# Attention and a mixer branch on one core: the first bit piece written from PSUM, twelve more shared blocks, and row-tile scores for some own key tiles

## The chip, the cores and the metric

The kernel runs on one NeuronCore of a Trainium2 chip. The metric is the device time of one execution in microseconds; lower is better. Before the change the median of three runs is 877.18 us (876.33 to 880.28). A core has five engines that run side by side and meet at semaphores: TensorE (PE, matrix products into PSUM), ScalarE (ACT, table functions such as exp and GELU), VectorE (DVE, elementwise work), GpSimd (POOL) and SyncE (SP, which here issues the DMA transfers). PSUM has eight banks of 512 fp32 columns on 128 partitions.

## The reference

```python
x  = A_x                                   # (1, 2048, 640) bf16
xn = layernorm(x)
# A: attention, 32 heads of 20
q, k, v = split(xn @ wqkv)                 # wqkv (640, 1920)
p = softmax(q @ k.T * 20**-0.5)            # 2048 x 2048 per head
s = concat_heads(p @ v) @ wo
# B: a mixer with two GELU products
h  = gelu(layernorm(xn) @ w1)              # four quarters of h are shifted by
hs = shift(h) @ w2                         # +1, -1, +2, -2 positions
x1 = xn + hs
g  = silu(x1 + gelu(layernorm(x1) @ w3) @ w4)   # w3 (640, 1536)
out = x + s * g
```

The exponentials are the bulk of it: 32 heads times 2048 x 2048 scores. On 128 partitions they are 1024 tiles of 128 x 1024.

## The kernel before

Heads are taken four at a time (a quad; eight of them), queries 512 at a time (a chunk; four per quad). Scores come with the keys on the partitions, so a key tile of 128 keys, with four heads and 512 queries, fills two PSUM tiles of 128 x 1024. For most key tiles ScalarE exponentiates both. A shared block is a pair of key tiles of which ScalarE takes one half and VectorE the other.

The kernel describes its work as tasks. A list scheduler inside the kernel, which runs when the program is built, puts the tasks of each engine into a fixed order, assigns PSUM banks and buffers, and adds the semaphore waits. `DUE` and some other numbers steer that order.

```python
self.RESERVE = 500.0
self.AHEAD = 3
# by number of shared blocks in a chunk: (position, block in unit, blocks of unit)
self.UNITS = ((),
              ((3, 0, 1),),
              ((0, 0, 2), (2, 1, 2)),
              ((0, 0, 2), (2, 1, 2), (7, 0, 1)),
              ((0, 0, 2), (1, 1, 2), (3, 0, 2), (5, 1, 2)))
self.ND = ([1, 2, 3, 3], [4, 4, 4, 3], [3, 3, 3, 2], [3, 3, 4, 3],   # shared blocks of
           [3, 2, 4, 2], [4, 3, 4, 4], [3, 3, 4, 3], [4, 4, 3, 1])   # each quad's chunks
# ...
EXP_B = (0.25, 32.25, 64.75, 96.75)
EXP_W = (1.0, 1.0, 181.0 / 256.0, 181.0 / 256.0)
EXP_BIAS = 31951.2055
# ... PSUM: bank 7 holds the weighted sum, banks 0 to 6 are shared
pairs = [(0, [0, 1]), (0, [2, 3])]
high = [(0, [4, 5]), (0, [5, 6]), (1, [4, 6])]
pl.kind("W", "B", [(0, [4]), (0, [6]), (1, [5])])             # projections, B branch
pl.kind("S", "B", pairs)                                      # one ScalarE tile
pl.kind("SD", "B", [(r + q, x + y) for r, x in pairs for q, y in high] + ...)
```

[...]a linear map of the score, read as a bf16 pattern, is 2 to a power with a linear mantissa. Four such patterns, shifted against each other by a fraction of an octave, two of them with a weight, add up to a smoother approximation. The sum is not formed on VectorE: each pattern (a piece) is a TensorE operand of its own, weighted through a scaled copy of V (`VP`). Before, the PSUM pass writes the linear map at twice the resolution into U, and each of four SBUF passes halves it and adds its piece's offset.

```python
def block_bits(self, quad, qc, blocks, ends):
    w = 2048 * len(blocks)
    # ...
    for v in range(4):
        k = self.piece % 3
        self.piece += 1
        dst, dsta = SS[:, k, 0:w], [A("SS", k)]
        T("dve", ..., lambda e, v=v, dst=dst: e.tensor_scalar(dst, U[:, ub, 0:w], 0.5, EXP_B[v], op0=ALU.mult, op1=ALU.add), ...)  # L1482
        for n, (j, kts) in enumerate(blocks):
            # four matmuls, one per head, each in its own column tile        # L1491
            ins = e.matmul(pb[32 * i:32 * i + 22, 0:512], wv, dst[:, at:at + 512].bitcast(BF16), ..., tile_position=(0, 32 * i))

def score(self, e, out, b, qc, kt, i):                     # row tile: 32 partitions of one head
    return e.matmul(out, self.KT[32 * i:32 * i + 32, b, 128 * kt:128 * kt + 128],
                    self.QT[32 * i:32 * i + 32, b, 512 * qc:512 * qc + 512],
                    start=True, stop=True, tile_position=(32 * i, 0))       # L1499

def score_act(self, b, qc, kt, a, gb=None):                # an own key tile, half a of two
    hs, sa = self.stile()
    def fn(e):
        for jj in range(2):
            out = self.bank(hs.slot + jj)
            if gb is None:                                 # first chunk of all: row tiles
                ins = self.score(e, out[:, :], b, qc, kt, 2 * a + jj)
                continue
            for c in range(4):                             # otherwise: QM is zero outside a head
                ins = e.matmul(out[32 * c:32 * c + 32, :], self.KT[:, b, 128 * kt + 32 * c:128 * kt + 32 * c + 32],
                               self.QM[:, gb, 2 * a + jj, :], start=True, stop=True, tile_position=(0, 32 * c))  # L1517
        return ins
    T("pe", ..., acq=("S", hs))
    return self.exp_act(hs, sa)                            # 128 x 1024 exponentials, L1541

def score_both(self, b, qc, kt, a, quad, r):               # half of a block: four row tiles at once
    # ... two heads to hs (ScalarE), two to hd (VectorE); four banks, acq=("SD", hs, hd)
    slot = self.exp_act(hs, sa)
    # the PSUM pass, L1568
    ins = e.tensor_scalar(U[:, ub, ...], self.psum[:, ...], a_exp, EXP_BIAS, op0=ALU.mult, op1=ALU.add)
```

Line numbers to know: L787 is every projection and B branch product; L1364 the weighted sum of ScalarE's tiles; L1405 the scores of the last chunk, which is done in two halves of 256 queries; L1603 takes a chunk's weighted sum out of PSUM; L1840 and L1911 are GELUs, L1927 the tanh of the gate.

Of the kernel before, what the change touches and what calls it, by code (L numbers as in the profile page):

```python
# [610 lines left out]
class Cfg:  # L611
# [5 lines left out]
    def __init__(self, S=2048, D=640, H=32, F=1536):  # L617
        self.S, self.D, self.H, self.F = S, D, H, F
        self.DH = D // H
        assert self.DH == 20 and D % 128 == 0 and F % 128 == 0 and S % 512 == 0  # L620
        self.NT = S // 128
        self.NQC = S // 512
        self.KC = D // 128
        self.FC = F // 128
        self.NQUAD = H // 4
        self.QW = 4 * self.DH
        self.scale = self.DH ** -0.5
        self.OFFSET = 60.0
        self.T0 = 38000.0
        self.STEP = 960.0  # L630
        self.DUE = dict(
            k0=-48.1, k1=-97.0, k2=-104.6, k3=-121.0, k4=-126.4, v0=25.8, v0s=11.55, v1=995.9, v1s=14.38, w1=349.3,
            w1s=18.63, g1=819.9, x1=141.8, x1s=0.43, wo=-14.8, st=92.5, g3_0=638.9, g3_2=540.7, si_0=348.9, si_2=654.6,
            sis=20.68, u0=4.5, s0=1.0, u1=3.5, s1=40.8, u2=-8.6, s2=51.1, u3=-29.2, s3=20.1, u4=-26.8, s4=-17.2, u5=-23.0,
            s5=-20.2, u6=-29.6, s6=-8.2, u7=-32.5, s7=170.4, mx=-11.2, mxs=3.13)
        self.BLK = [(2, 3), (6, 7), (10, 11), (14, 15)]
        self.RESERVE = 500.0
        self.POOLN = [0, 9, 14]
        self.HPE = 0.0
        self.HDVE = 0.0  # L640
        self.THIRD = False
        self.FALL = True
        self.SAVE = 1
        self.AHEAD = 3
        self.UNITS = ((),
                      ((3, 0, 1),),
                      ((0, 0, 2), (2, 1, 2)),
                      ((0, 0, 2), (2, 1, 2), (7, 0, 1)),
                      ((0, 0, 2), (1, 1, 2), (3, 0, 2), (5, 1, 2)))
        self.HPS = 6  # L650
        self.FILL = 0
        self.LNA = [3, 3]
        self.VAFTER = 6
        self.NPF = [34, 8]
        self.TRA = [1, 2, 3, 4, 8, 13, 17, 18]
        self.ONP = 0
        self.LAST = [[[4, 2]], []]
        self.ND = (
            [1, 2, 3, 3],
            [4, 4, 4, 3],  # L660
            [3, 3, 3, 2],
            [3, 3, 4, 3],
            [3, 2, 4, 2],
            [4, 3, 4, 4],
            [3, 3, 4, 3],
            [4, 4, 3, 1])

    def order(self, quad, qc):

        nb = self.ND[quad][qc]
        used = [k for b in self.BLK[:nb] for k in b]
        ks = [k for k in range(self.NT) if k not in used]
        at = {}
        for j, (pos, r, n) in enumerate(self.UNITS[nb]):
            at.setdefault(pos, []).append(("b", j, r, n))
        out = []
        for i in range(len(ks) + 1):
            out += at.pop(i, [])  # L680
            if i < len(ks):
                out.append(("k", ks[i]))
        assert not at
        return out

# [1 line left out]

EXP_B = (0.25, 32.25, 64.75, 96.75)  # L690
EXP_W = (1.0, 1.0, 181.0 / 256.0, 181.0 / 256.0)
EXP_BIAS = 31951.2055


def c_dve(n, kind="psum"):
# [11 lines left out]
def c_act(n):  # L707
    return 68 + 0.8333 * n
# [13 lines left out]
class Gen:  # L722
# [71 lines left out]
    def build(self, plan_only=False):  # L794
        nc, pl = self.nc, self.pl
        with contextlib.ExitStack() as es:
# [13 lines left out]
            pl.kind("S", "B", pairs + (third if self.cfg.THIRD else []))  # L810
            pl.kind("SD", "B", [(r + q, x + y) for r, x in pairs for q, y in high]
                    + ([(3, pairs[0][1] + pairs[1][1]), (3, pairs[1][1] + pairs[0][1])] if self.cfg.FALL else []))
            pl.hold = {"pe": self.cfg.HPE, "dve": self.cfg.HDVE}
            if self.cfg.SAVE:
                pl.saves = {"SD": "W"}
                pl.reserve = self.cfg.RESERVE
                pl.hard = self.cfg.SAVE == 2
            pl.pool("PT", 7)
            self.program()
            ms = pl.schedule(verbose=True)  # L820
            if plan_only:
# [497 lines left out]
    def attn_quad(self, quad):  # L1319
# [9 lines left out]
        for qc in range(NQC):  # L1329
# [17 lines left out]
            for kind, x, *unit in seq:  # L1347
                if kind == "k":
                    slots = [self.score_act(b, qc, x, a, gb if col else None) for a in range(2)]
                    kts = (x, x)  # L1350
                else:
                    ka, kb = kts = cfg.BLK[x]
                    r, n = unit
# [22 lines left out]
    def last_half(self, quad, qc, half, gb):  # L1376
# [40 lines left out]
        for x, kt in enumerate(ks):  # L1417
# [9 lines left out]
            for unit in at.get(x, []):  # L1427
# [3 lines left out]
                for m, kx in enumerate(unit):  # L1431
                    hs, sa = scores(kx, "d")
                    T("dve", c_dve(1024),
                      lambda e, m=m, hs=hs, ub=ub: e.tensor_scalar(U[:, ub, 1024 * m:1024 * m + 1024], self.psum[:, 512 * hs.slot:512 * hs.slot + 1024],
                                                                   cfg.scale * math.log2(math.e) * 256.0, EXP_BIAS, op0=ALU.mult, op1=ALU.add),
                      reads=[sa], writes=[A("U", ub, m)], name=f"uh{half}_{kx}", rel=hs, cls=-1 - half, due=self.at(self.nact, f"u{quad}"))
                for v in range(4):
                    k = self.piece % 3
                    self.piece += 1
                    T("dve", c_dve(w, "4x"),  # L1440
                      lambda e, v=v, k=k, ub=ub, w=w: e.tensor_scalar(SS[:, k, 0:w], U[:, ub, 0:w], 0.5, EXP_B[v], op0=ALU.mult, op1=ALU.add),
                      reads=[A("U", ub, m) for m in range(len(unit))], writes=[A("SS", k)], name=f"s_h{half}_{unit[0]}_{v}", cls=-2 * half,
                      due=self.at(self.nact, f"s{quad}"))
                    for m, kx in enumerate(unit):
                        own = EXP_W[v] == 1.0
                        T("pe", c_pe(4, 256), pv(vown if own else (lambda j, i: VX[:, j // 2, i, :]), kx,
                                                 lambda i, k=k, m=m: SS[:, k, 1024 * m + 256 * i:1024 * m + 256 * i + 256].bitcast(BF16)),
                          reads=[A("SS", k), A("VX") if not own else A(f"VA{hf}", kx), pva], name=f"pvd_h{half}_{kx}_{v}", cls=-half)
            T("pe", c_pe(4, 256), pv(vown, kt, lambda i, hp=hp: PT[:, hp.slot, 256 * i:256 * i + 256]), reads=[pa, A(f"VA{hf}", kt), pva], rel=hp,
              name=f"pv_h{half}_{kt}", cls=-1)  # L1450
        RZ, Ob, h8 = self.RZ, self.Ob, 8 * half
# [16 lines left out]
    def block_bits(self, quad, qc, blocks, ends):  # L1468
# [7 lines left out]
        self.unit += 1  # L1476
        halves = [A("U", ub, k) for k in range(2 * len(blocks))]
        for v in range(4):
            k = self.piece % 3
            self.piece += 1  # L1480
            dst, dsta = SS[:, k, 0:w], [A("SS", k)]
            T("dve", c_dve(w, "4x"), lambda e, v=v, dst=dst: e.tensor_scalar(dst, U[:, ub, 0:w], 0.5, EXP_B[v], op0=ALU.mult, op1=ALU.add),  # L1482
              reads=halves, writes=dsta, name=f"s{quad}_{qc}_{blocks[0][0]}_{v}", due=self.at(self.nact, f"s{quad}"))
            for n, (j, kts) in enumerate(blocks):
                def fn(e, v=v, dst=dst, n=n, j=j, kts=kts):
                    pb = self.bank(self.PVB)
# [15 lines left out]
    def score_act(self, b, qc, kt, a, gb=None):  # L1502
# [19 lines left out]
          writes=[sa, ("turn", self.step)], name=f"sc{self.step}", mode=int(gb is None), cls=-1, acq=("S", hs))  # L1522
        return self.exp_act(hs, sa)

    def stile(self):
        h = Handle()
        a = ("S", h.id)
# [19 lines left out]
    def score_both(self, b, qc, kt, a, quad, r):  # L1547
# [4 lines left out]
        U, ub = self.U, self.unit % 2  # L1552
        o = 1 - a
        at = 2 * r + o
        a_exp = cfg.scale * math.log2(math.e) * 256.0
        (hs, sa), (hd, da) = self.stile(), self.stile()
        def fn(e):
            for i in range(4):
# [410 lines left out]
```

## Time and profile before

| | before |
|---|---|
| time, median of three | 877.18 us |
| span of the profiled run | 873.5 us |
| TensorE matmuls | 16078, busy 830.2 us |
| VectorE busy | 732.3 us |
| ScalarE busy | 837.9 us |
| first exponential starts | 36.9 us |
| mean granted TensorE clock | 0.993 |

Busy time is how long an engine had an instruction in flight. On TensorE instructions overlap and their ends are modelled, so its share doesn't tell how much room is left; the distance from the start of one instruction to the start of the next does. A row of the groups gives line, engine and operation, output and input shapes, count, then busy microseconds and mean nanoseconds of one, then the idle time of the engine ahead of it and what ended it. In a list of waits the numbers are microseconds in total, times, and the longest one. In the chain that ended last each stretch belongs to the work that the next one had to wait for.

### The profile page before, as it was taken

How to read it: one execution, taken by the hardware profiler on the slowest of the kernel's cores; microseconds unless marked ns; L12 is line 12 of the kernel's file. 1: busy time of each engine (PE TensorE's matmuls, PEld its weight loads, DVE VectorE, ACT ScalarE, POOL GpSimd, SP SyncE). 2: the span in 40 equal slices, each digit the busy share in tenths (PEclk: the TensorE clock that was granted, in tenths of full speed). 3: DMA queues.
4: the chain of work that ended last, by engine and by line, in shares of the span. 5: the costliest groups of instructions: out<-in, count | busy, mean ns of one | idle time of the engine just before them, and what ended most of it. 6: DMA issues, size and time to landing. Idle time of an engine off the chain costs nothing.

```text
span 873.5 us, 35127 instructions
## 1 busy us (share of the span) xinstructions
PE 830.2 (95%) x16078; PEld 373.4 (43%) x16078; DVE 732.3 (84%) x1006; ACT 837.9 (96%) x887; POOL 43.6 (5%) x74
## 2 busy tenths in 40 slices
PE   7899989999999999999999999999998999999996
PEld 3334333333344444443444545444333344443485
DVE  7746779999879998889886599799997778899957
ACT  7699999999999999999999999999999999999994
POOL 7600000000000000000110000000000000000000
PEclk9999999999999999999999999999999999999998
DMA  7001533222130001331323112232221202013232
GB/s 227 17 2 36 130 88 88 77 84 84 57 92 13 26 26 45 104 75 35 76 53 99 32 55 84 78 98 53 61 52 46 60 26 70 25 48 113 84 95 92
DMA packets 86483, 59.06 MB, mean 68 GB/s; under 512 B 53056, under 2 KB 77840, under 8 KB 86336
## 3 DMA queue, kind: packets, MB, share of 16 engines
q1 hardware_dynamic: 86336, 56.82, 23.6%
q8 instruction: 126, 2.06, 1.0%
q14 instruction: 21, 0.17, 0.1%
HBM read 42.10 MB, written 10.63 MB: 60 GB/s over the span
## 4 chain that ended last, share of the span: by engine, by line
ACT 74%; PE 16%; DVE 7%; DMA 2%; issue 1%; SPq 0%
ACT arena L1541 70%; PE psum L787 6%; PE psum L1517 3%; ACT arena L1911 2%; PE psum L1499 2%; PE psum L1405 2%; PE psum L1364 1%; DVE arena L1568 1%; DVE arena L1482 1%; PE psum L1491 1%; ACT arena L1927 1%; DMA queries<-arena 1%; DMA arena<-in_A_x_dram 1%; DMA recips<-arena 1%; DVE arena L1199 1%
## 5 line engine op out<-in xcount | busy, mean ns | idle before, releaser
L1541 ACT ACTIVATE arena<-psum 128x1024 bf16<-128x1024 f32 x826 | 769.1, 1038 | 9.5 <-PE psum L1499 3.4
L787 PE MATMUL psum<-arena 128*32 128x320 bf16 (+1 forms) x5952 | 358.3, 333 | 6.0 <-DVE arena L1201 3.0
L1517 PE MATMUL psum<-arena 128*32 128x512 bf16 x4576 | 348.2, 381 | 7.8 <-ACT arena L1541 6.5
L1568 DVE TENSOR_SCALAR arena<-psum 128x1024 uint16<-128x1024 f32 x196 | 238.7, 1218 | 39.4 <-PE psum L1499 39.0
L1482 DVE TENSOR_SCALAR arena<-arena 128x4096 uint16<-128x4096 uint16 (+1 forms) x228 | 238.1, 1070 | 3.6 <-PE psum L1491 2.5
L787 PEld LDWEIGHTS psum<-arena 128*32 128x32 bf16 x5952 | 148.2, 96 | 138.4 <-issue 25.8
L1517 PEld LDWEIGHTS psum<-arena 128*32 128x32 bf16 x4576 | 97.3, 95 | 130.8 <-ACT arena L1541 93.5
L1364 PE MATMUL psum<-arena 128*22 128x512 bf16 x1592 | 152.0, 380 | 0.8 <-DVE arena L1603 0.6
L1491 PE MATMUL psum<-arena 128*22 128x512 bf16 x1568 | 129.1, 380 | 0.6 <-DVE arena L1482 0.6
L1499 PE MATMUL psum<-arena 32*128 32x512 bf16 x840 | 88.0, 385 | 13.0 <-ACT arena L1541 6.8
L1499 PEld LDWEIGHTS psum<-arena 32*128 32x128 bf16 x840 | 22.4, 91 | 102.1 <-ACT arena L1541 80.9
L1364 PEld LDWEIGHTS psum<-arena 128*22 128x22 bf16 x1592 | 40.3, 92 | 49.1 <-issue 6.8
L1491 PEld LDWEIGHTS psum<-arena 128*22 128x22 bf16 x1568 | 36.6, 92 | 43.5 <-issue 8.6
L1907 DVE CAST arena<-psum 128x512 bf16<-128x512 f32 x48 | 32.8, 684 | 11.6 <-PE psum L787 10.1
L1245 DVE CAST arena<-psum 128x512 bf16<-128x512 f32 x40 | 27.3, 685 | 18.1 <-PE psum L787 17.9
L1691 DVE SCALAR_TENSOR_TENSOR arena<-psum,arena 128x320 bf16<-128x320 f32 x32 | 15.4, 486 | 13.8 <-PE psum L787 13.7
L1922 DVE TENSOR_TENSOR arena<-psum,arena 128x320 bf16<-128x320 f32 x32 | 15.5, 485 | 13.3 <-PE psum L787 12.2
L999 DVE BATCH_NORM_STATS2 arena<-arena 128x6 f32<-128x320 bf16 x52 | 22.9, 480 | 3.3 <-DMA arena<-in_A_x_dram 3.2
L1314 POOL TENSOR_SCALAR arena<-arena 128x176 bf16<-128x176 bf16 x16 | 8.5, 534 | 326.1 <-DVE arena L1306 326.0
L1306 DVE CAST arena<-psum 128x320 bf16<-128x320 f32 x32 | 15.1, 487 | 10.9 <-PE psum L787 10.9
L1603 DVE COPY arena<-psum 128x512 f32<-128x512 f32 x28 | 19.2, 685 | 2.7 <-PE psum L1491 1.7
L1616 DVE TENSOR_TENSOR arena<-arena 128x512 bf16<-128x512 f32 x28 | 19.1, 683 | 2.1 <-DMA arena<-recips 2.1
(118 smaller groups left out, 349.1 us busy)
## 6 DMA issues: line engine op xcount, KB each, us to landing
arena<-in_B_w_dram SPq DMA_DIRECT2D x48, 160.0 KB, 2.6
arena<-recips SPq DMA_DIRECT2D x28, 256.0 KB
arena<-arena SPq DMA_DIRECT2D x124, 32.0 KB, 1.9
arena<-in_B_w_dram SPq DMA_DIRECT2D x4, 960.0 KB, 5.8
arena<-in_A_x_dram SPq DMA_DIRECT2D x8, 320.0 KB, 6.2
arena<-in_A_x_dram SPq DMA_DIRECT2D x16, 160.0 KB, 2.5
out_dram<-arena SPq DMA_DIRECT2D x16, 160.0 KB, 1.9
heads<-arena SPq DMA_DIRECT2D x112, 20.0 KB
```

The costliest lines, as they stand in the source:

```text
L787: ins = e.matmul(pb[32 * c:32 * c + 32, 0:N], lhsT(k, c), rhs(k, c), start=(k == 0), stop=(stop and k == nk - 1), tile_position=(0, 32 * c))
L999: lambda e, li=li, n=n, hh=hh: e.bn_stats(st[:, li, 6 * hh:6 * hh + 6], xn[:, n, hD * hh:hD * hh + hD]),
L1245: T("dve", c_dve(512), lambda e, h=h, c=c: e.tensor_copy(KS[:, 512 * c:512 * c + 512], self.wbank(h)[:, 0:512]), reads=[wa], writes=[A("KS ...
L1364: ins = e.matmul(pb[32 * i:32 * i + 22, 0:512], VA[:, ql, kts[i // 2], i, :], PT[:, slots[i // 2][0].slot, 512 * (i % 2):512 * (i % 2) + 512],
L1482: T("dve", c_dve(w, "4x"), lambda e, v=v, dst=dst: e.tensor_scalar(dst, U[:, ub, 0:w], 0.5, EXP_B[v], op0=ALU.mult, op1=ALU.add), reads=ha ...
L1491: ins = e.matmul(pb[32 * i:32 * i + 22, 0:512], wv, dst[:, at:at + 512].bitcast(BF16), start=first, stop=final, tile_position=(0, 32 * i))
L1499: return e.matmul(out, self.KT[32 * i:32 * i + 32, b, 128 * kt:128 * kt + 128], self.QT[32 * i:32 * i + 32, b, 512 * qc:512 * qc + 512], s ...
L1517: ins = e.matmul(out[32 * c:32 * c + 32, :], self.KT[:, b, 128 * kt + 32 * c:128 * kt + 32 * c + 32], self.QM[:, gb, 2 * a + jj, :], start ...
L1541: lambda e: e.activation(self.PT[:, hp.slot, :], self.psum[:, 512 * hs.slot:512 * hs.slot + 1024], AF.Exp, scale=cfg.scale),
L1568: ins = e.tensor_scalar(U[:, ub, 1024 * at + 512 * k:1024 * at + 512 * k + w], self.psum[:, 512 * hd.slots[k]:512 * hd.slots[k] + w], a_ex ...
L1603: T("dve", c_dve(512), lambda e: e.tensor_copy(Ob[:, :], self.bank(self.PVB)[:, :]), writes=[("PV", 0), A("Ob")], name=f"ob{quad}_{qc}", c ...
L1907: T("dve", c_dve(512), lambda e, h=h, fc=fc, i=i: e.tensor_copy(GT[:, i, fc, :], self.wbank(h)[:, 0:512]), reads=[wa], writes=at, name=f"g ...
```

## The change

Four things change together. The linear map is written at single resolution, with the first piece's offset in it, so the PSUM pass yields the first piece itself: TensorE reads it straight from U, and three SBUF passes, each a single add, make the other three. Shared blocks go from 98 to 110, so VectorE takes 24 more of the 1024 tiles and ScalarE 24 fewer. 39 own key tiles (outside the first chunk) take their scores in one set of four row tiles, as blocks do, instead of 16 matmuls against QM: 31 of them with two exponentials of 1024, and eight ("w") with one exponential of 2048 over four adjacent banks. And the numbers that steer the scheduler are other ones, so the order of tasks is another one nearly everywhere. In the first chunk no block is shared any more.

```diff
-            k0=-48.1, k1=-97.0, k2=-104.6, ...
+            k0=553.73, k1=-179.82, k2=-347.19, ...
...
-        self.RESERVE = 500.0
+        self.RESERVE = 350.0
...
-        self.AHEAD = 3
+        self.AHEAD = 2
...
+        self.NR = (
+            [[], [12, 110, 113], [5, 11, 105, 108, 112, 114], [3, 6, 9, 10, 11, 106, 112, 114]],
...
         self.ND = (
-            [1, 2, 3, 3],
-            [4, 4, 4, 3],
-            [3, 3, 3, 2],
-            [3, 3, 4, 3],
-            [3, 2, 4, 2],
+            [0, 4, 4, 3],
+            [4, 4, 4, 4],
+            [3, 2, 4, 4],
             [4, 3, 4, 4],
-            [3, 3, 4, 3],
-            [4, 4, 3, 1])
+            [3, 4, 4, 4],
+            [4, 3, 4, 4],
+            [3, 4, 4, 4],
+            [4, 4, 2, 3])
...
+        rows = self.NR[quad][qc]
...
-                out.append(("k", ks[i]))
+                out.append(("r" if i in rows else "w" if 100 + i in rows else "k", ks[i]))
...
-EXP_B = (0.25, 32.25, 64.75, 96.75)
+EXP_B = (0.0, 32.0, 64.0, 96.0)
 EXP_W = (1.0, 1.0, 181.0 / 256.0, 181.0 / 256.0)
-EXP_BIAS = 31951.2055
+EXP_BIAS = 15975.95
...
+            pl.kind("SR", "B", [(r + q, x + y) for r, x in pairs for q, y in high[:2]]
+                    + [(3, pairs[0][1] + pairs[1][1]), (3, pairs[1][1] + pairs[0][1])])
+            pl.kind("SW", "B", [(0, [2, 3, 4, 5])])
...
         for v in range(4):
-            k = self.piece % 3
-            self.piece += 1
-            dst, dsta = SS[:, k, 0:w], [A("SS", k)]
-            T("dve", c_dve(w, "4x"), lambda e, v=v, dst=dst: e.tensor_scalar(dst, U[:, ub, 0:w], 0.5, EXP_B[v], op0=ALU.mult, op1=ALU.add),
-              reads=halves, writes=dsta, name=f"s{quad}_{qc}_{blocks[0][0]}_{v}", due=self.at(self.nact, f"s{quad}"))
+            if v == 0:
+                dst, dsta = U[:, ub, 0:w], halves
+            else:
+                k = self.piece % 3
+                self.piece += 1
+                dst, dsta = SS[:, k, 0:w], [A("SS", k)]
+                T("dve", c_dve(w, "4x"), lambda e, v=v, dst=dst: e.tensor_scalar(dst, U[:, ub, 0:w], EXP_B[v], None, op0=ALU.add),
+                  reads=halves, writes=dsta, name=f"s{quad}_{qc}_{blocks[0][0]}_{v}", due=self.at(self.nact, f"s{quad}"))
...
+    def score_rows(self, b, qc, kt, wide):
+        tiles = [self.stile() for _ in range(2)]
+        def fn(e):
+            for i in range(4):
+                ins = self.score(e, self.bank(tiles[i // 2][0].slots[i % 2])[:, :], b, qc, kt, i)
+            return ins
+        T("pe", 220, fn, ..., acq=("SW" if wide else "SR",) + tuple(h for h, _ in tiles))
+        if not wide:
+            return [self.exp_act(h, a) for h, a in tiles]
...
+        T("act", c_act(2048),
+          lambda e: e.activation(self.PT[:, hp[0].slot:hp[0].slot + 2, :], self.psum[:, 512 * h0.slot:512 * h0.slot + 2048]...,
+                                 AF.Exp, scale=self.cfg.scale), ...)
...
-        a_exp = cfg.scale * math.log2(math.e) * 256.0
+        a_exp = cfg.scale * math.log2(math.e) * 128.0
```

## The prediction

> **What bounds the kernel now.** I read the page's first part, then the chain that ended last, then ScalarE's waits, then the costly groups, then TensorE in order of time.
>
> ```profile
> PE 830.2 (95%) x16078; PEld 373.4 (43%) x16078; DVE 732.3 (84%) x1006; ACT 837.9 (96%) x887; POOL 43.6 (5%) x74
> ...
> ACT 74%; PE 16%; DVE 7%; DMA 2%; issue 1%; SPq 0%
> ```
>
> ScalarE is busy for 96% of the span and is 74% of the chain. TensorE's 95% is not a margin read directly, because matmuls overlap in the records; I come back to it. ScalarE's waits, from first exponential to last (37 to 860 us):
>
> ```profile
> ACT arena L1541 <- PE psum L1499: 3.4, 7, 1.1
> ACT arena L1541 <- PE psum L1364: 3.0, 3, 2.1
> ACT arena L1541 <- PE psum L1405: 2.0, 1, 2.0
> ACT arena L1541 <- PE psum L1517: 0.5, 2, 0.4
> ```
>
> In those 823 us ScalarE is busy for 813.9 and waits 9 us, always for TensorE. By windows, 4.2 us of it lie between 100 and 200 us, 2.1 us at 420 to 440 and 2.0 us at 820 to 840. So an exponential taken from ScalarE is worth nearly its whole slot, as long as TensorE and VectorE keep up. The groups:
>
> ```profile
> L1541 ACT ACTIVATE arena<-psum 128x1024 bf16<-128x1024 f32 x826 | 769.1, 1038 | 9.5 <-PE psum L1499 3.4
> ...
> L1568 DVE TENSOR_SCALAR arena<-psum 128x1024 uint16<-128x1024 f32 x196 | 238.7, 1218 | 39.4 <-PE psum L1499 39.0
> ```
>
> One exponential lasts 1038 ns, but 826 of them make 769.1 us of busy time: they overlap, and the slot is 769.1 / 826 = 931 ns. The bit passes, shapes kept apart:
>
> ```profile
> L1482 DVE TENSOR_SCALAR arena<-arena 128x4096 uint16<-128x4096 uint16 x164 | 196.3, 1219 | 2.7 <-PE psum L1491 2.0
> L1482 DVE TENSOR_SCALAR arena<-arena 128x2048 uint16<-128x2048 uint16 x64 | 41.8, 687 | 0.9 <-PE psum L1491 0.5
> ```
>
> TensorE in order of time, around a row-tile set (L1499); the first column is the start:
>
> ```profile
> 502.43 0.60 PE L1517 MATMUL psum<-arena 128*32 128x512 bf16 x8
> 502.86 0.39 PE L1364 MATMUL psum<-arena 128*22 128x512 bf16 x4
> 503.07 0.39 PE L787 MATMUL psum<-arena 128*32 128x512 bf16 x4
> 503.40 0.39 PE L1499 MATMUL psum<-arena 32*128 32x512 bf16 x4
> 503.72 0.61 PE L787 MATMUL psum<-arena 128*32 128x512 bf16 x8
> ```
>
> Four concurrent column-tile matmuls of 512 columns take one place of 0.43 / 2 = 0.215 us. From the set ahead of the row-tile set to it are 0.33 us, and from it to the next 0.32: about 0.105 us extra at each change of tiling, so a lone row-tile set costs 0.43 us.
>
> **What the Trainium skill says.** "TensorEngine Tiling (Array Packing)", Key Properties: a change of tiling mode drains TensorE. The 0.105 us above is that cost here. The same page, Gotcha 1, says that different row tiles write different PSUM banks, so a row-tile set needs four banks free at once; the profile of before can't show what that costs an own key tile, as none is made that way after the first query chunk. "ScalarE: Activation LUTs", What ACT_TABLE_LOAD costs, gives an ACTIVATE as 186 ns + 0.833 per element, with 93 ns of overlap: 1039 ns alone and 946 in sequence for 1024 elements; the trace has 1038 and 931. "VectorE: DVE Perf Modes", The perf-mode tier table, has tensor_scalar over 2048 bf16 in SBUF at 693 ns (4x) and slower from PSUM; the trace has 687, and 1218 for 1024 fp32 from PSUM. The new add keeps 16-bit SBUF operands and constants, so I give it the same time.
>
> **The change, part by part.** Counts are from the instruction streams of both kernels.
>
> ScalarE: shared blocks go from 98 to 110. A block hands two 1024-wide tiles to VectorE, so exponentials fall from 826 to 802 tiles: 24 x 0.931 = 22.3 us less. Sixteen of the 802 become eight of 2048, which each save the fixed part of a slot, 931 - 1024 x 0.833 = 78 ns: 0.6 us. ScalarE loses 22.9 us, all on the path.
>
> VectorE: 24 more PSUM passes (four of these now in halves) cost 24 x 1.218 = 29.2 us. Bit passes fall from 164 to 156 of 4096 and from 64 to 18 of 2048: 8 x 1.219 + 46 x 0.687 = 41.4 us less. The last chunk's split unit saves one more pass of 0.7. Net -12.9, before the passes' small overlaps; I take -10. So VectorE does 12 more blocks within its old time: that part is the enabler, not the gain. Reading the piece from U also frees a staging buffer, but holds U until TensorE has read it.
>
> TensorE: QM-form score matmuls fall from 4576 to 3664 (-228 sets), row-tile ones rise from 840 to 1068 (+57), own weighted sums fall from 1592 to 1544 (-12), bit sums rise from 1568 to 1760 (+48): -135 sets x 0.215 = -29 us. Visits to row tiling rise from 224 (196 halves of blocks, 28 tiles of the first chunk) to 291 (220, 32, and 39 own key tiles: 31 narrow, 8 wide): 67 x 0.21 = +14 us. Net -15 us. The scores of an own key tile fall from 16 matmuls in four places, 0.86 us, to 0.43.
>
> So the three move by -23, -10 and -15. The loads of TensorE and ScalarE relative to each other matter. I walked both instruction streams, cut them after each query chunk's last weighted sum, and gave each set its place (0.215 for 512 columns, 0.136 for 320, 0.109 for 256, 0.055 for 128, 0.105 per change of tiling) and each ScalarE instruction its slot; a quad is four chunks. From the first exponential on, TensorE against ScalarE, cumulated in us:
>
> Before: quad 0 98.9 against 102.4; quad 1 187 against 194; quad 3 388 against 399; end 781 against 816.
> After: quad 0 99.7 against 98.7; quad 1 199 against 199; quad 3 379 against 385; end 764 against 793.
>
> Before, TensorE has some 3 to 5% of slack throughout, and still ScalarE lost 4 us by 200 us. After, it has none in the first two quads: the B branch's first product is pulled forward (its GELU stands after 163 tiles instead of 217), while the saving from row tiles comes later. Later its slack is 3 to 4%, as before. If TensorE runs at 96 to 98% of its places there, 199 becomes 203 to 207, and ScalarE idles 4 to 8 us by the end of quad 1. I add 1 us for the middle and 2 for the last chunk, where TensorE's 29 us stand against ScalarE's 28. That is 9 us on average, with a tail upward: 10.5 us against 9 before, or 1.5 us given back.
>
> Start and end: the same instructions stand before the first exponential, except that one VectorE pass (L960, 2.0 us, on the chain at 27.6 us) moves behind the key bound. It may give a microsecond; I count nothing. The end after the last exponential (13 us) is unchanged.
>
> Sum: 877.2 - 22.9 + 1.5 = 855.8; I say 855.5.
>
> **The rivals.** First, TensorE as the bound: it gains only 15 us, and early it gains nothing. For it: ScalarE waits only for TensorE, and the totals of the first two quads are level. Against: from quad 2 on there is as much slack as before. If it bound all through, the time would be 877 - 15 = 862. Second, PSUM banks: 39 row sets need four of seven banks at once, a wide one holds four through a 1.78 us exponential, and projections share three of them. For it: VectorE already waits 39 us for row-tile scores. Against: these are few (39 x about 0.2 us = 8 us if each stalls ScalarE), and they are placed between tiles that own other banks. That would give 863. Third, VectorE: 16 of quad 1's 16 blocks. It was full from 160 to 200 us before. Now a four-block chunk takes 8 x 1.22 + 6 x 1.22 = 17.1 us of bits against ScalarE's 24 x 0.931 = 22.3, where before it took 19.5; so I expect no bound there. If the add lost the 4x rate, 174 passes would each take about twice as long, some 175 us more, and the kernel would be far slower; the existing 16-bit pass with one constant (L1211, 1024 elements in 419 ns) speaks against that.
>
> **Range and chances.** Nearly all of the gain is a count times a measured slot; the uncertainty is how much ScalarE idles. Idle of 4 us gives 849, 18 us gives 863. I take 849 to 864. Faster by over 2% means under 859.6 us, idle of up to about 14 us: 0.84. Within 2%: 0.14. Slower: 0.02.
>
> **What would show it.** ScalarE's busy time near 815 and its span share at 95 to 96%; 802 tiles in slots of 931 ns; bit passes still at 1219 ns; VectorE busy near 722; ScalarE's waits 8 to 14 us, mostly before 220 us and for TensorE. It is wrong if these waits exceed 15 us, if the waits name row-tile scores after 250 us (the banks), or if the add's duration changes.

## The result and the profile after

The changed kernel takes 864.84 us (median of four runs, 864.0 to 866.92); the kernel before took 876.75 us in the runs beside it (874.46 to 880.28). The ratio is 0.9868, with a 95% interval of 0.9839 to 0.9896: 1.3% faster, where 2.5% was predicted, and just above the range of 849 to 864 us.

One count of the change has to be set right first. 31 own key tiles take their scores in one row-tile set, 23 of them with two exponentials and eight wide; I had taken the 31 for the narrow ones alone and so came to 39. The matmuls against QM show it, after and in run e11 below, which takes these sets out: 4160 - 3664 = 496, and an own key tile has 16.

```profile
L1542 PE MATMUL psum<-arena 128*32 128x512 bf16 x3664 | 278.9, 381 | 10.9 <-ACT arena L1589 9.2
```

```profile
L1540 PE MATMUL psum<-arena 128*32 128x512 bf16 x4160 | 318.2, 382 | 4.8 <-ACT arena L1587 4.2
```

The first part of the profile after and its chain by engine:

```profile
PE 813.6 (94%) x15538; PEld 362.4 (42%) x15538; DVE 723.7 (84%) x977; ACT 818.7 (95%) x855; POOL 41.9 (5%) x74
...
PE 51%; ACT 36%; DVE 10%; DMA 1%; issue 1%; POOL 1%; SPq 0%; DVEq 0%; POOLq 0%
```

The busy times are close to what was predicted: VectorE 723.7 us against 722, ScalarE 818.7 against 815. But the chain has changed sides. Before it was 74% ScalarE and 16% TensorE; now it is 36% and 51%. The line map: the exponentials are L1589 (wide ones L1566), scores against QM L1542, row-tile scores L1524, the scores of the last chunk L1423, the weighted sum of ScalarE's tiles L1382, the sum of the bit pieces L1516, VectorE's PSUM pass L1616, its bit passes L1507, products L797.

The waits of ScalarE after (total microseconds, times, longest):

```profile
ACT arena L1589 <- PE psum L1524: 12.9, 32, 0.7
...
ACT arena L1589 <- PE psum L1542: 2.5, 5, 1.1
ACT arena L1589 <- PE psum L1423: 2.3, 2, 1.9
...
ACT arena L1589 <- PE psum L1382: 0.7, 3, 0.2
```

Seven waits for row-tile scores, 3.4 us, have become 32 and 12.9 us. They are short (0.4 us on average) and spread over the whole run; after 250 us there are still 7.3 us of them:

```profile
ACT arena L1589 <- PE psum L1524: 7.3, 19, 0.7
```

A wait for a weighted sum (L1382 here) is one for a buffer: each sum frees one of the seven buffers that ScalarE's results go to. The groups after that answer to those of before, forms kept apart:

```profile
L1589 ACT ACTIVATE arena<-psum 128x1024 bf16<-128x1024 f32 x786 | 736.2, 1035 | 20.3 <-PE psum L1524 12.9 <-PE psum L1542 2.5 <-PE psum L1423 2.3
...
L1566 ACT ACTIVATE arena<-psum 128x2048 bf16<-128x2048 f32 x8 | 15.1, 1890 | 0.0
```

```profile
L1616 DVE TENSOR_SCALAR arena<-psum 128x1024 uint16<-128x1024 f32 x218 | 265.2, 1217 | 43.3 <-PE psum L1524 41.7
L1507 DVE TENSOR_SCALAR arena<-arena 128x4096 uint16<-128x4096 uint16 x156 | 185.7, 1215 | 0.8
```

The single add over 4096 values takes 1215 ns, the old multiply-and-add took 1219: its rate is kept. The slot of an exponential is 736.2 / 786 = 937 ns, against 931 before.

From both traces, the span divides into three parts (the first and the last exponential bound the middle one):

| us | before | after | difference |
|---|---|---|---|
| first exponential starts | 36.9 | 39.4 | +2.6 |
| first exponential to end of last | 823.9 | 815.0 | -8.9 |
| of it ScalarE idle | 8.6 (14 stalls) | 19.3 (54 stalls) | +10.7 |
| from there to the end | 12.7 | 8.4 | -4.3 |
| span of the profiled run | 873.5 | 862.9 | -10.6 |

The end is shorter because of work that is no longer left over. Before, TensorE in order of time around the last exponential's end (860.8 us):

```profile
860.95 0.28 PE L1395 MATMUL psum<-arena 128*22 128x256 bf16 x4
...
861.06 3.84 PE L787 MATMUL psum<-arena 128*32 128x320 bf16 x108
```

After, where the last exponential ends at 854.4 us:

```profile
854.50 0.29 PE L1413 MATMUL psum<-arena 128*22 128x256 bf16 x4 [0.36 <-ACT arena L1589]
...
854.61 0.44 PE L1751 MATMUL psum<-arena 128*32 128x320 bf16 x8
```

Before, 108 matmuls of the output product, 3.84 us, stood behind the last weighted sum; after, they are done by then. This comes from the new order.

One of the short stalls in order of time. It begins with a half of a block at 140.71 whose four scores lie in the four low banks, that is, in two of ScalarE's pairs; VectorE's tile has taken one of them:

```profile
140.71 0.39 PE L1524 MATMUL psum<-arena 32*128 32x512 bf16 x4
...
141.44 1.21 DVE L1616 TENSOR_SCALAR arena<-psum 128x1024 uint16<-128x1024 f32 x1
...
142.36 0.39 PE L1524 MATMUL psum<-arena 32*128 32x512 bf16 x4 [0.52 <-ACT arena L1589]
...
142.81 1.02 ACT L1589 ACTIVATE arena<-psum 128x1024 bf16<-128x1024 f32 x1 [0.50 <-PE psum L1524]
```

With one pair lent out ScalarE has no second tile to go on with. The next set can't begin before the running exponential has given its pair back (the 0.52 us wait of the set), and ScalarE then waits for that set (0.50 us). I counted the sets over the four low banks in both programs: 1 before, 15 after, ten of them halves of blocks and five own key tiles. The stalls at such a set or at the tile behind it make up 7.0 us in 13 stalls after (2.4 us in 4 of them at own key tiles), 1.0 us in 2 before; one more of 0.5 us comes in the last chunk, where VectorE also takes one of ScalarE's pairs. That is 7.5 us in 14 stalls. Of the others 29, 9.4 us, are tiles whose banks were free while TensorE still had other work in its order ahead of them, 9 of 1.9 us waited for banks that VectorE held, and 2 of 0.5 us for a bank of ScalarE's own. This sorting is mine, from the banks in the programs and the times in the traces.

### The profile page after: what moved, and what is told of

Same layout as the page of the kernel before. It is cut to its first block, busy times and chain, and to the rows that moved or that the text cites. A ratio compares the mean times of both kernels' runs of the same rounds, so it can differ in the third digit from the quotient of the medians.

```text
span 862.9 us, 33979 instructions
## 1 busy us (share of the span) xinstructions
PE 813.6 (94%) x15538; PEld 362.4 (42%) x15538; DVE 723.7 (84%) x977; ACT 818.7 (95%) x855; POOL 41.9 (5%) x74
## 4 chain that ended last, share of the span: by engine, by line
PE 51%; ACT 36%; DVE 10%; DMA 1%; issue 1%; POOL 1%; SPq 0%; DVEq 0%; POOLq 0%
ACT arena L1589 31%; PE psum L797 17%; PE psum L1542 12%; PE psum L1524 7%; PE psum L1382 6%; PE psum L1516 5%; DVE arena L1616 4%; ACT arena L1959 2%; DVE arena L1507 2%; PE psum L981 1%; ACT arena L1888 1%; DMA shifts<-arena 1%; ACT arena L1566 1%; PE psum L1120 1%; DVE arena L1260 1%
## 5 line engine op out<-in xcount | busy, mean ns | idle before, releaser
L1589 ACT ACTIVATE arena<-psum 128x1024 bf16<-128x1024 f32 x786 | 736.2, 1035 | 20.3 <-PE psum L1524 12.9
L797 PE MATMUL psum<-arena 128*32 128x320 bf16 (+1 forms) x5952 | 351.6, 333 | 5.4 <-DVE arena L1216 2.2
L1616 DVE TENSOR_SCALAR arena<-psum 128x1024 uint16<-128x1024 f32 (+1 forms) x222 | 267.8, 1207 | 44.3 <-PE psum L1524 42.8
L1542 PE MATMUL psum<-arena 128*32 128x512 bf16 x3664 | 278.9, 381 | 10.9 <-ACT arena L1589 9.2
L797 PEld LDWEIGHTS psum<-arena 128*32 128x32 bf16 x5952 | 148.0, 96 | 133.2 <-issue 28.8
L1507 DVE TENSOR_SCALAR arena<-arena 128x4096 uint16<-128x4096 uint16 (+1 forms) x174 | 197.4, 1160 | 1.0
L1382 PE MATMUL psum<-arena 128*22 128x512 bf16 x1544 | 148.2, 381 | 2.9 <-ACT arena L1589 2.6
L1516 PE MATMUL psum<-arena 128*22 128x512 bf16 x1760 | 141.2, 380 | 0.7 <-DVE arena L1507 0.4
L1542 PEld LDWEIGHTS psum<-arena 128*32 128x32 bf16 x3664 | 80.0, 95 | 102.4 <-ACT arena L1589 70.4
L1524 PE MATMUL psum<-arena 32*128 32x512 bf16 x1068 | 111.1, 384 | 12.1 <-ACT arena L1589 6.0
L1524 PEld LDWEIGHTS psum<-arena 32*128 32x128 bf16 x1068 | 28.3, 91 | 121.2 <-ACT arena L1589 74.0
L1382 PEld LDWEIGHTS psum<-arena 128*22 128x22 bf16 x1544 | 38.5, 91 | 60.1 <-issue 16.8
L1516 PEld LDWEIGHTS psum<-arena 128*22 128x22 bf16 x1760 | 42.9, 92 | 48.1 <-issue 8.4
L1321 DVE CAST arena<-psum 128x320 bf16<-128x320 f32 x32 | 15.4, 488 | 18.2 <-PE psum L797 18.0
L1959 ACT ACTIVATE arena<-arena 128x12288 bf16<-128x12288 bf16 x2 | 20.9, 10446 | 0.0
L981 PE MATMUL psum<-arena 128*32 128x512 bf16 x168 | 12.8, 463 | 7.3 <-POOL arena L947 6.4
```

The costliest lines, as they stand in the source:

```text
L797: ins = e.matmul(pb[32 * c:32 * c + 32, 0:N], lhsT(k, c), rhs(k, c), start=(k == 0), stop=(stop and k == nk - 1), tile_position=(0, 32 * c))
L1382: ins = e.matmul(pb[32 * i:32 * i + 22, 0:512], VA[:, ql, kts[i // 2], i, :], PT[:, slots[i // 2][0].slot, 512 * (i % 2):512 * (i % 2) + 512],
L1589: lambda e: e.activation(self.PT[:, hp.slot, :], self.psum[:, 512 * hs.slot:512 * hs.slot + 1024], AF.Exp, scale=cfg.scale),
L1616: ins = e.tensor_scalar(U[:, ub, 1024 * at + 512 * k:1024 * at + 512 * k + w], self.psum[:, 512 * hd.slots[k]:512 * hd.slots[k] + w], a_ex ...
L1959: T("act", 2750 + c_act(2 * FC * 512), lambda e: e.activation(GT[:, :, :, :], GT[:, :, :, :], AF.Gelu_apprx_tanh), reads=gta, writes=gta, ...
```

## The experiments

**Which engine's order is the floor.** The first theory was that TensorE's order is now the bound, and that what was taken from ScalarE lies on top of it; the rivals were VectorE, which returns banks late, and the later start. The following kernels keep the changed kernel's order, waits and instruction counts, and make one engine's instructions shorter. They leave out part of the computation.

Run e1 leaves out three quarters of the columns of the B branch's, the second V projection's and the output product (TensorE's busy time falls from 813.6 to 747.0 us):

```diff
+                n = N // 4 if name[:2] in ("v1", "w1", "w2", "w3", "w4", "wo") else N
-                    ins = e.matmul(pb[32 * c:32 * c + 32, 0:N], lhsT(k, c), rhs(k, c), ...
+                    ins = e.matmul(pb[32 * c:32 * c + 32, 0:n], lhsT(k, c), rhs(k, c)[:, 0:n], ...
```

> The changed kernel with the same tasks, order, buffers and waits, but every product of the B branch, of the second V projection and of the output streams a quarter of its columns: three quarters of these products are left out. By the places measured before (0.215 us for 512 columns, 0.136 for 320) TensorE loses some 130 us, about 16 of it before 200 us. Theory 1 (TensorE had no slack in the first two quads, and ScalarE's 19.7 us of waits between its first and last exponential are TensorE's backlog): the waits fall to under 5 us, and the time to about 848. Theory 2 (the waits come from PSUM banks: a row-tile set waits until VectorE's pass, or the ScalarE tile before, has given its banks back): at least 12 us of waits stay, above all ScalarE for the row-tile scores, and the time stays above 855.

Measured: 857.58 us, 7.3 us less than after. Its chain and its first wait:

```profile
ACT 64%; DVE 18%; PE 13%; DMA 2%; issue 1%; SPq 0%; DVEq 0%
```

```profile
ACT arena L1590 <- PE psum L1525: 12.7, 29, 0.7
```

By its numbers the second theory came true (at least 12 us of waits, above 855 us) and the first did not. TensorE's share of the chain falls from 51% to 13%, but ScalarE's idle time stays at 18.2 us: the stalls behind TensorE's own order fall from 9.4 to 3.2 us, and in their place tiles wait for banks that VectorE returns (7.1 us, before 1.9), while those at low-bank sets stay at 7.2 us. The time fell all the same, so neither theory alone holds: TensorE is a bound, and VectorE lies just behind it.

Run e2 leaves out three quarters of the columns of nearly all VectorE PSUM passes (VectorE's busy time falls from 723.7 to 568.9 us):

```diff
+                key = (ub, at, k, w)
+                if key in SEEN:
+                    w = 256 if w == 1024 else 128
+                SEEN.add(key)
```

> The changed kernel with the same order and waits, but VectorE's PSUM pass covers a quarter of its columns after the first use of each part of its buffer (three quarters of the linear map are left out): about 0.4 us instead of 1.22, so VectorE's banks come back 0.8 us sooner, 222 times. Theory 1 (TensorE's backlog): ScalarE's waits stay within 3 us of the 19.7 of the changed kernel, the time within 3 us of 864.8. Theory 2 (banks given back late by VectorE): ScalarE's waits fall below 10 us and the time to 853 to 857.

Measured: 861.25 us, 3.6 us less than after. ScalarE idles 18.0 us in 47 stalls, 9.9 us of them behind TensorE's own order. The waits are as the first theory said, the time 0.6 us beyond its range; VectorE alone is not the cause.

Run e5 does both:

> The changed kernel, same order and waits, with both lightenings at once: products of the B branch, second V projection and output on a quarter of their columns, and VectorE's PSUM pass on a quarter of its columns. With the products alone 18.2 us of ScalarE waits stayed (five of them newly ended by VectorE's pass), with the pass alone 18.0 (ten us still behind TensorE's queue). Theory A (two limits lie on top of each other: TensorE's queue, and VectorE giving its banks back; beside them a fixed part of about 7.5 us, where a block half took both ScalarE pairs of banks): the waits fall to 8 to 12 us, and nearly all that stay follow a set over banks 0 to 3; time 846 to 853. Rival (each wait is ScalarE's own bank pair coming back): the waits stay above 15 us.

Measured: 851.58 us, 13.3 us less than after, more than the 10.9 us of the two alone. Its chain and its first wait for row-tile scores (L1535):

```profile
ACT 79%; PE 15%; DVE 2%; DMA 1%; POOL 1%; issue 1%; SPq 0%; DVEq 0%; POOLq 0%
```

```profile
ACT arena L1600 <- PE psum L1535: 7.7, 17, 0.6
```

Only now is ScalarE the bound, as the prediction had it for all of the changed kernel, and the time is 4 us below the predicted one. It still idles 13.2 us, more than the 8 to 12 expected, and 6.8 us of it in 13 stalls, half and not nearly all, lie at low-bank sets and at the last chunk's lent pair.

Run e3 shortens the exponentials instead, to half their columns (a slot's first one excepted); ScalarE's busy time falls to 543.9 us, and TensorE and VectorE run in their order as fast as they can:

```diff
-               lambda e: e.activation(self.PT[:, hp.slot, :], self.psum[:, 512 * hs.slot:512 * hs.slot + 1024], AF.Exp, ...
+               lambda e: e.activation(self.PT[:, hp.slot, 0:short(hp.slot)], self.psum[:, 512 * hs.slot:512 * hs.slot + short(hp.slot, True)], AF.Exp, ...
```

> The changed kernel with the same order and waits, but each exponential covers half of its columns after the first use of its buffer: about 0.6 us instead of 1.035, some 340 us of ScalarE's work left out. It shows what the other engines and the order allow. Theory 1 (TensorE without slack): the time falls by less than 25 us, to 840 or more, and TensorE is the chain. Theory 2 (bank handover between TensorE, VectorE and ScalarE): each handover also gets shorter by half an exponential, so the time falls further, to between 800 and 840.

Measured: 853.1 us, only 11.7 us below after, although ScalarE has 275 us less to do: the first theory's outcome. Its chain:

```profile
PE 67%; DVE 27%; ACT 2%; DMA 1%; issue 1%; POOL 1%; SPq 0%; DVEq 0%; POOLq 0%
```

**The same two cuts on the kernel before.** Run e6 is e1's cut and e7 is e3's, made in the kernel before.

> The kernel before, same order and waits, with the same products on a quarter of their columns. Theory (before, ScalarE set the pace alone and TensorE had 3 to 5% of slack): of 8.6 us of ScalarE waits only about 4 go, and the time falls by 2 to 6 us, to 871 to 875, less than the 7.3 us of the changed kernel. Rival (TensorE set the pace before as well): the time falls by more than 8 us.

> The kernel before, same order and waits, with exponentials on half of their columns, as was done to the changed kernel, where the time fell by only 11.7 us to 853.1. It measures what TensorE, VectorE and the order allow without ScalarE. If that floor is TensorE's work (15 us of places more than after), the time is 866 to 871, within 10 us of before, and the change could never have brought much more than the floor moved. If the kernel before had real slack, it is below 856.

Measured: e6 869.77 us, e7 867.89 us (two runs, 3 us to either side), beside 877.57 us of the kernel before in the same comparison. In e6 the fall of 7.8 us lies between the theory's 2 to 6 and the rival's 8, and is no less than in e1; e7 is inside its range for a floor of TensorE's work. The chain of e7:

```profile
PE 59%; DVE 33%; DMA 3%; ACT 3%; issue 2%; POOL 0%; SPq 0%; POOLq 0%
```

This is the reading that the profile of before didn't give. Taking 277 us from ScalarE, 74% of the chain, brought 9.7 us. From the first exponential to the last, e7 takes 819.2 us and the kernel before 823.9; after has 804.2 (e3) and 815.0. In these two traces the floor without ScalarE's load moved by -15.0 us. How far exactly is open: e7's profile is of the longer of its two runs (870.95 us; the other took 864.84), so 8 to 15 us is what the runs allow. The floor isn't TensorE's alone either: VectorE is a quarter to a third of both chains.

**The start.** In the profile after, a bitwise AND over 512 values on VectorE (L1166) lies across GpSimd's memsets. VectorE:

```profile
33.38 2.95 DVE L1166 TENSOR_SCALAR arena<-arena 128x512 uint16<-128x512 uint16 x1
```

GpSimd over the same time:

```profile
31.37 1.81 POOL L973 MEMSET arena<- 128x2048 bf16 x1
33.11 1.81 POOL L974 MEMSET arena<- 128x2048 bf16 x1
...
34.94 1.25 POOL L1314 MEMSET arena<- 128x256 bf16 x1
```

The same pass took 0.28 us before. It stands ahead of the key bound and so of the first exponential. The Trainium skill, "SBUF — State Buffer", section "SBUF: two separate sides", says that VectorE in a two-port mode and GpSimd take a shared port pair as a lock for whole instructions; the traces agree. In e2, e3 and e5, which leave the start as it is, the pass took 1.65, 1.69 and 1.37 us and ended 0.15 us after the memset that it had started beside; in the profile above it stayed blocked through the following ones as well. Run e4 makes the memsets from L973 on wait until the key bound is formed; all else is as in the changed kernel:

```diff
+            by = {t.name: t for t in pl.tasks}
+            assert by["mq_"].signals
+            pl.waits[by["kt0"].id].append((sems["dve"], by["mq_"].seq))
```

> The changed kernel with one wait more: GpSimd's two memsets of the second K and Q buffers stand until VectorE has made the key bound's mask. Nothing is left out and no order changes. Theory of the late start: in the changed kernel VectorE's 16-bit pass over 512 columns at 33.4 us took 2.95 us instead of 0.28 as these memsets and the ones behind them ran (the Trainium skill, SBUF — State Buffer, SBUF: two separate sides: VectorE in a two-port mode and GpSimd share a port pair under an exclusive lock), so the first exponential starts at 36.5 to 37.2 us instead of 39.4 and the time falls by 2 to 3 us, to about 862.3. Rival (the start is late because of the order of TensorE's projections): the pass becomes short, and the first exponential still starts after 38.5 us.

Measured: 866.24 us (ratio to before 0.9899, 0.9865 to 0.9934). The pass and the first exponential did as they should; VectorE in e4:

```profile
31.77 0.29 DVE L1169 TENSOR_SCALAR arena<-arena 128x512 uint16<-128x512 uint16 x1
...
35.71 2.26 DVE L978 TENSOR_SCALAR arena<-arena 128x2048 bf16<-128x2048 bf16 x1 [1.90 <-POOL arena L976]
```

The pass takes 0.29 us and the first exponential starts at 35.7 us, 3.7 us earlier. Of these 1.6 us are not the memsets' doing, as the pass itself begins at 31.77 instead of 33.38 us. The time didn't fall as expected: the last exponential ends at 854.3 us, as in after (854.4), and ScalarE idles 22.2 us instead of 19.3. Its lead is lost again in waits, and no cost of the later start can be seen. Part of the +2.6 us of the table is scatter, too: in e2 and e3 the first exponential starts at 37.9 and 37.7 us.

**The parts of the change.** Run e8 makes the new form of the bit pieces alone in the kernel before: U at single resolution, three adds, everything else and all steering numbers of the kernel before.

```diff
-EXP_B = (0.25, 32.25, 64.75, 96.75)
+EXP_B = (0.0, 32.0, 64.0, 96.0)
...
+            if v == 0:
+                dst, dsta = U[:, ub, 0:w], halves
```

> The bit part alone on the kernel before: the PSUM pass writes the first piece into U, three passes add to it; 98 blocks, no own row-tile sets, and the old steering numbers. 57 bit passes and about 60 us of VectorE's work go. Theory (VectorE's time was no bound; the new durations go into the scheduler, whose steering numbers were fitted to the old ones, so the order gets worse): slower than before, 885 to 900, ScalarE busy as before near 838 and its waits above 25 us. Rival (VectorE's lighter load frees banks and staging sooner): 872 to 877.

Measured: 900.15 us, ratio 1.0258 (1.0228 to 1.0288): slower, though VectorE is busy for 682.3 us instead of 732.3. Where it goes, in ScalarE's waits:

```profile
ACT arena L1548 <- PE psum L1364: 26.8, 9, 7.5
```

The waits are few and long, for buffers: weighted sums that would free them stand late in TensorE's order. For the longest wait the scores begin at 501.50 us, but the sum comes only after 68 and 56 matmuls of projections and products, and ScalarE goes on at 509.68 us:

```profile
501.50 0.60 PE L1524 MATMUL psum<-arena 128*32 128x512 bf16 x8
...
502.80 3.85 PE L787 MATMUL psum<-arena 128*32 128x512 bf16 x68
...
509.24 0.82 PE L1364 MATMUL psum<-arena 128*22 128x512 bf16 x12
```

The list scheduler had put the tasks into another order because VectorE's were shorter. Run e9 is the same kernel, with only the `DUE` numbers fitted anew by a search over the scheduler's own plan:

```diff
-            k0=-48.1, k1=-97.0, k2=-104.6, k3=-121.0, k4=-126.4, ...
+            k0=123.01, k1=-76.54, k2=-107.17, k3=3.94, k4=-104.84, ...
```

> The kernel before with the new form of the bit pieces alone (blocks, own key tiles and ScalarE's 826 tiles as before), but with the scheduler's DUE numbers fitted anew to it. Theory: the new form only makes room on VectorE (busy near 682 us instead of 732), and ScalarE and TensorE keep their whole load, so the time stays within 1% of before: 870 to 882 us; the 900 us of the same part under the old numbers is then an effect of the order alone. Rival one: the part itself costs (U is held until TensorE has read it), then 890 us or more again. Rival two: VectorE's late return of banks cost the kernel before much, then 868 us or less.

Measured: 883.08 us, ratio 1.0073 (1.0044 to 1.0102), a microsecond above the theory's range. So 17 us of e8's loss was the order. Whether the last 6.7 us over before are order too, or the longer hold of U, these runs don't tell: of its 15.7 us of idle, some 14 us lie behind TensorE's own order. Fifty microseconds freed on VectorE brought nothing by themselves.

Run e10 takes the 31 row-tile sets of own key tiles out of the changed kernel, and leaves its steering numbers; e11 takes them out and fits `DUE` anew. Bits and 110 blocks stay, and so do ScalarE's 802 tiles, all as 1024-wide exponentials.

```diff
-                out.append(("r" if i in rows else "w" if 100 + i in rows else "k", ks[i]))
+                out.append(("k", ks[i]))
```

> The changed kernel without its 39 own key tiles by row-tile sets (they go through QM as the others), under the steering numbers of the changed kernel, not fitted anew. Theory: TensorE carries 39 x 0.43 = 17 us more and the order no longer fits, so 875 us or more. Rival: only ScalarE's number of tiles counts, then 865 us.

> The same without row-tile sets for own key tiles, with DUE fitted anew. ScalarE's 802 tiles of 1024 stay, so by the prediction's ScalarE term alone the time would be 865 us as in the changed kernel. Theory (TensorE's load lies right below ScalarE's): TensorE carries 17 us more than after, so about 869 to 876 us, that is, the twelve blocks then gain 1% at most, and ScalarE waits for QM scores (L1540) and sums and not for row tiles after 250 us. Rival (the row sets themselves are what makes ScalarE stall, through the banks): 858 to 864 us, ScalarE's waits under 10 us.

Measured: e10 885.63 us (one run); e11 875.36 us (median of twenty runs), ratio 0.9984 (0.9974 to 0.9995) to before. The chain of e11:

```profile
PE 56%; ACT 33%; DVE 8%; DMA 1%; issue 1%; POOL 1%; DVEq 0%; POOLq 0%
```

and ScalarE's waits after 250 us in e11, QM scores being L1540 there, row-tile scores L1522 and weighted sums L1380:

```profile
ACT arena L1587 <- PE psum L1540: 9.8, 14, 3.1
ACT arena L1587 <- PE psum L1522: 4.8, 11, 0.8
ACT arena L1587 <- PE psum L1380: 3.2, 2, 2.2
```

Both theories gave the right range, though on 17 us; with 31 sets TensorE carries 31 x 0.43 = 13 us more. With 24 exponentials less than before, e11 is 0.16% faster: the 22 us taken from ScalarE come back whole as idle time (30.6 us from the first to the last exponential, 8.6 before), mostly in waits for QM scores and sums. Row-tile waits are still there, from the halves of blocks, but fewer. The rival, that the row sets themselves are what makes ScalarE stall, falls as the main cause. TensorE's work goes with the time of both kernels. By the places of the prediction, e11 has 3 us less of it than before (42 sets fewer, 28 visits to row tiling more) and takes 1.0 us less time; the changed kernel has 17 us less and takes 11.9 us less. This speaks for the row-tile sets, which relieve TensorE, as what makes the 10.5 us between e11 and the changed kernel, but doesn't prove it: e11's order was fitted by a short search, and e9, fitted in the same way, came out 6.7 us above before, so more than half of the 10.5 us could be order.

Run e12 asks for the cost of the sets over the four low banks: they are forbidden, steering and block counts fitted anew (108 blocks, so that ScalarE has 806 tiles, and 28 own key tiles by row sets, of which 8 wide; the 36 below repeats the miscount).

```diff
-                    + ([(3, pairs[0][1] + pairs[1][1]), (3, pairs[1][1] + pairs[0][1])] if self.cfg.FALL else []))
+)
...
-            pl.kind("SR", "B", [(r + q, x + y) for r, x in pairs for q, y in high[:2]]
-                    + [(3, pairs[0][1] + pairs[1][1]), (3, pairs[1][1] + pairs[0][1])])
+            pl.kind("SR", "B", [(r + q, x + y) for r, x in pairs for q, y in high[:2]])
```

> The changed kernel with no set over the four low banks allowed for a half of a block (nor for a narrow own key tile), steering and block counts fitted anew (108 blocks, 36 own key tiles by row sets). Theory: the stalls of 0.5 us of ScalarE behind such sets (14 in the changed kernel, 7.7 us) are gone, so that its waits for row-tile scores fall from 12.9 us to about 5 us, but halves of blocks wait for VectorE's own banks instead, so the time isn't better: 870 to 882 us. Rival: the stalls for row tiles come from every set of four banks, then the waits for row tiles stay above 10 us in some 30 stalls of about 0.4 us.

Measured: 879.65 us (one run). The waits:

```profile
ACT arena L1586 <- PE psum L1521: 19.9, 30, 4.0
ACT arena L1586 <- PE psum L1539: 6.4, 11, 1.2
```

A miss as a test. The time is in the theory's range, but the waits for row tiles rose to 19.9 us in 30 stalls instead of falling to 5. By the letter that is the rival's sign; but single waits of 4.0 us, ten times the rival's, show another order, so the run decides for neither. What a low-bank set costs in an order that is otherwise the same wasn't measured: the 7.5 us rest on the sorting of the trace and on their persistence in e1 and e5.

## Why the prediction was wrong

**The step that failed** is "So an exponential taken from ScalarE is worth nearly its whole slot, as long as TensorE and VectorE keep up", and with it the term for ScalarE's idle time, "10.5 us against 9 before, or 1.5 us given back". The condition in that sentence was already at its limit. The prediction read ScalarE's small waits and its 74% of the chain as distance to the next bound. Run e7 shows the distance: before, with ScalarE's load cut by a third, TensorE and VectorE still need 819.2 us from the first exponential to the last (an estimated 813 in the shorter run, if its 6 us lie there), where ScalarE's busy time is 815.2 and the kernel takes 823.9. Two limits lay on top of each other, and a chain names only one of them.

**The sizing behind it.** The table of TensorE's places gave 781 us before and 764 after, and I took TensorE to run at 96 to 98% of its places, only in the first two quads. Relieved of ScalarE's load it reaches 781 / 819.2 and 764 / 804.2: 95% both times, over the whole run, its waits for VectorE included. The floor after is thus 804 us, above ScalarE's 793, so "3 to 4% of slack" after the second quad was none.

**The counts.** With 31 own key tiles and not 39 there are 59 more visits to row tiling and not 67: -29 + 59 x 0.21 = -17 us for TensorE and not -15, which is also what the table's 781 and 764 give. The forecast didn't rest on the slip: its sum has ScalarE's terms alone, and the table was taken from the instruction streams. (Of VectorE's 24 added PSUM passes two are in halves, not four.)

**The middle part, term by term.** Predicted -22.9 + 1.5 = -21.4 us, measured -8.9. ScalarE's idle time rose by 10.7 us instead of 1.5. Its busy time in that stretch (length less idle) fell from 815.2 to 795.7, by 19.5 instead of 22.9: an exponential that starts after a stall has no predecessor to overlap with and takes 1038 instead of 931 ns, so 40 more stalls cost up to 40 x 0.107 = 4.3 us. 9.2 + 3.4 = 12.6 us, which is the difference but for rounding. Seen from the other side: the floor fell by 8 to 15 us, and some 6 us more were lost at low-bank sets (7.5 against 1.0). Whether the floor alone makes the -8.9, or a larger fall less these stalls, the runs don't tell, as e7 scatters by 6 us and e12 did not isolate the stalls.

**Start and end.** "I count nothing" and "unchanged" were +2.6 and -4.3 us. Run e4 shows that the first matters little. The second shows in the trace: the output product is off the tail.

**What held.** 802 tiles; VectorE's net of -10 (732.3 to 723.7); the rate of the add; the blocks being "the enabler, not the gain" for VectorE's time. But in e11 blocks and bits together gained next to nothing without the row-tile sets, which the prediction had as a side effect.

**The rivals.** The first, TensorE binding all through, 877 - 15 = 862, was right in kind and 3 us off; the argument against it ("as much slack as before") took a slack that wasn't there. The second, banks, had 863 and the right line in the waits, but named only some of the sets: of the 7.0 us at low-bank sets 2.4 us lie at own key tiles, the rest at the halves of blocks that borrow ScalarE's pair. The third, VectorE, binds only where TensorE is relieved (e1 against e5). Two of the three signs that I had named for being wrong came in: idle above 15 us, and row-tile scores after 250 us.

## What to carry to other kernels

Where two engines are both busy for over 90%, the chain shows which one ended last, not how far the other is behind; halving the columns of one engine's instructions in the same order measures it, and is worth doing before work is moved away from that engine. A part that only frees an engine below the bound (here the bit pieces, 50 us on VectorE) or moves work off one of two equal limits (the blocks) brought next to nothing here while the other limit stood. Numbers that steer a scheduler belong to one set of task lengths: a part tried alone under numbers fitted to another kernel can look 17 us worse than it is.

## What the runs showed of the hardware

A VectorE pass of 0.28 us over 16-bit data in SBUF took 1.37 to 2.95 us beside GpSimd's memsets (after, e2, e3, e5), and 0.29 us when they were held back (e4); a pass that then met the memsets took 2.26 us instead of 0.78. A stall of ScalarE costs more than its own length: up to 0.107 us of overlap between two exponentials of 1024 (1038 ns each, 931 ns in sequence) goes with it. And in both runs in which the exponentials were halved (e3 and e7), the places of TensorE's matmuls added up to 95% of the time that its order took (764 of 804.2 us, 781 of 819.2), the waits for VectorE included.
